# Attention values of the later batches: a float32 product with the values stationary in column tiles, and the weights summed on GpSimd

## The chip, the cores and the metric

The kernel runs on one core of a Trainium2 chip. The metric is device time in microseconds (us) for one execution: 2009.07 us before the change, the median of three runs (2008.14 to 2009.09). PE is the matrix engine (TensorE), ACT is ScalarE, DVE is VectorE, POOL is GpSimd, and SP is the queue that issues the transfers.

## The reference, cut to what matters

Four batches of 12480 tokens with 128 channels each. 49 agents first attend to all keys, and then every query attends to the 49 agents:

```python
a2k = softmax(scale * agents @ k.T)      # 49 x 12480, per batch
agent_v = a2k @ v                        # 49 x 128
q2a = softmax(scale * q @ agents.T)      # 12480 x 49
x = q2a @ agent_v                        # tokens x 128
out = (relu(x @ w_in) ** 2) @ w_out      # w_in 128 x 2048, w_out 2048 x 128
```

A softmax subtracts the row's maximum and divides by the sum of the exponentials plus 1e-9. The change is in `a2k @ v` and in the sum of the exponentials that belongs to it, for batches 1 to 3.

## The kernel before

Everything is done transposed: channels or agents on partitions, tokens along the free dimension. `agent_v @ w_in` is one table of 49 x 2048 per batch (`tables`, L327), so that a token's hidden row is its 49 query weights times the table. Tables, weights and hidden values are split into a high and a low float32r part, so that products of float32r come out with float32 accuracy.

**The main loop** (L575) runs over 832 slots. A slot is one eighth of the hidden width for one half (480 tokens) of a block of 960 tokens. Two slots make a pair, and the loop works in pairs. For pair p, counted from 0:

- `first` (L402): PE makes two hidden tiles `h`, one for the even and one for the odd slot, each of two halves of 128 x 480. The pool of `h` has three tiles.
- `hidden` (L420): ACT makes `r` (relu of `h`) and `g_hi` (its square, rounded); DVE multiplies `r` and `h` into `gg`. For an even slot, `gg` is a tile of its own (two of them) and its low part `g_lo = gg - g_hi` is made on POOL in two halves (L433); for an odd slot the product stays in `h` and DVE makes `g_lo`. So the even `h` is free after DVE's `gg`, the odd one after DVE's `g_lo`.
- `second` (L445): the output products, three times two matmuls for each slot (`g_hi` by `wo_hi`, `g_hi` by `wo_lo`, `g_lo` by `wo_hi`), four slots later (`LAG`), that is after `first` of pair p+2.

These instructions are put in a fixed chain for each engine (`queued`, L56). Everything else in the main loop is fed in as steps of two generators and placed between them by a scheduler, which fixes each engine's order when the program is built; at run time each engine works through its own list in order and waits at the head.

- `queries` (L352) makes the query weights of the next block: scores on PE, exponentials, normalisation (`e`, `z`), the split on ACT and POOL (`pp`), four transposes twice (L382).
- `background` (L462) prepares the next batch: `scores` for 13 blocks of keys (12 of 1024 keys, one of 192), `maxima`, then `values` for the same 13 blocks, `gathered`, `tables`. `STEPS` (L481) says how many steps that is, and sets its pace: the steps of a batch are spread over 0.88 of the slots of the batch before.

Small products that don't belong to the main chain write to one single bank of PSUM (`bank`, L156): key scores, query scores, transposes, values and tables follow each other there, and each waits until the one before has been read.

`scores` keeps the scores of a block in a tile `s` of its own (13 tiles, one for each block) and a running maximum in `mx`. `maxima` makes one maximum per agent and spreads it over all partitions (`mb`, L231). `tiled` (L178) is a float32 product whose stationary operand is cut into four column tiles of 32.

`values` (L288), before: POOL subtracts the maximum into `d` (two buffers), ACT takes the exponential, ACT and POOL split the 128 x 392 weights into high and low parts side by side (`e`, two buffers), and the 128 x 1024 values likewise (`vs`, two buffers, with a column of ones for the sum of the weights). PE then multiplies with the weights as the stationary operand (98 columns: both parts) and the values as the moving one (258 columns: both parts and the ones), eight float32r matmuls a block (L303), and DVE adds the result to `av`. `gathered` (L311) adds up the four quarters with a matrix product with `quad`.

Batch 0 has no earlier batch to hide behind. It runs ahead of the main loop with `whole_exps`, `whole_values`, `add_weights` and `whole_sums` (L246 to L286): exponentials in place in `s`, a plain float32 product, the weights summed into `mx` on POOL, and one sum over partitions at the end.

Of the kernel before, what the change touches and what calls it, by code (L numbers as in the profile page):

```python
# [9 lines left out]
F32 = mybir.dt.float32  # L10
F32R = mybir.dt.float32r
U32 = mybir.dt.uint32
AF = mybir.ActivationFunctionType
ALU = mybir.AluOpType
# [3 lines left out]
P = 128  # L18
TP = 120
NT = 8  # L20
# [17 lines left out]
def agent_attention_relu2(ctx: ExitStack, tc: tile.TileContext, qT, kT, v, agT, w_in, w_out, outT):  # L38
    nc = tc.nc
    C, NTOK = qT.shape  # L40
    _, B, NA = agT.shape
    N = NTOK // B
    FF = w_in.shape[1]
# [3 lines left out]
    NK = len(blocks)  # L47
    K2 = 2 * NA
# [3 lines left out]
    scale = 1.0 / math.sqrt(C)  # L52
# [22 lines left out]
    pe, act, dve, pool, sync = (Ordered(e) for e in (nc.tensor, nc.scalar, nc.vector, nc.gpsimd, nc.sync))  # L75

    const = ctx.enter_context(tc.tile_pool(name="const", bufs=1))
    kv = ctx.enter_context(tc.tile_pool(name="kv", bufs=2))
    sp = ctx.enter_context(tc.tile_pool(name="sp", bufs=NK))
    small = ctx.enter_context(tc.tile_pool(name="small", bufs=1))  # L80
# [10 lines left out]
    ident = const.tile([P, P], F32, name="ident")  # L91
# [1 line left out]
    identr = const.tile([TP, TP], F32R, name="identr")  # L93
    nc.scalar.copy(identr, ident[:TP, :TP])

    quad = const.tile([K2, 2, NA], F32, name="quad")
    nc.gpsimd.tensor_copy(quad, ident[:K2, :K2].rearrange("p (h a) -> p h a", h=2))
    for base in (NA, -NA):
        nc.gpsimd.affine_select(
            out=quad.rearrange("p h a -> p (h a)"), in_=quad.rearrange("p h a -> p (h a)"),  # L100
            pattern=[[-1, K2]], compare_op=ALU.not_equal, fill=1.0, base=base, channel_multiplier=1,
        )

    split = [const.tile([P, NT, 2 * (C + 1)], F32R, name=f"vs{i}") for i in range(2)]
    for vs in split:
        nc.gpsimd.memset(vs[:, :, C : C + 1].bitcast(F32), 1.0)
        nc.gpsimd.memset(vs[:, :, 2 * C + 1 :].bitcast(F32), 0.0)
    win = const.tile([C, FF], F32, name="win")
    wo_hi = const.tile([P, NCH, C], F32R, name="wo_hi")
    wo_lo = const.tile([P, NCH, C], F32R, name="wo_lo")  # L110
# [45 lines left out]
    def bank():  # L156
        if alone[0]:
            return ps_h.tile([P, 2, 512], F32, name="h")[:, 0, :]
        return ps_a.tile([P, 512], F32, name="psa")
# [3 lines left out]
    state = {}  # L163

    def load_keys(b, i, pool, name):
        at, rows, nt = blocks[i]
        kt = pool.tile([C, KB], F32, name=name)
        sync.dma_start(kt[:, : rows * nt], kT[:, b * N + at : b * N + at + rows * nt])
        return kt

    def load_values(b, i, pool, name):
        at, rows, nt = blocks[i]
        vt = pool.tile([P, KB], F32, name=name).rearrange("p (t c) -> p t c", c=C)
        src = v[b, at : at + rows * nt, :].rearrange("(p t) c -> p t c", p=rows)
        sync.dma_start(vt[:rows, :nt, :], src)
        return vt

    def tiled(out, stationary, moving):  # L178
        n = stationary.shape[1]
        with tc.high_priority():  # L180
            for at in range(0, n, CT):
                up = min(at + CT, n)
                pe.matmul(out[at:up, :], stationary[:, at:up], moving, start=True, stop=True)  # L183

    def scores(b, i, kt):
        st = state.setdefault(b, {"s": []})
# [27 lines left out]
    def maxima(b):  # L214
        st = state[b]
        m1 = small.tile([P, NA], F32, name="m1")
        dve.reduce_max(m1, st["mx"].rearrange("p t a -> p a t"), axis=AX.X)
        yield
        pt = bank()
        pe.transpose(pt[:NA, :P], m1, ident)  # L220
        yield
        m2 = small.tile([NA, 1], F32, name="m2")
        dve.reduce_max(m2, pt[:NA, :P], axis=AX.X)
        dg = small.tile([NA, NA], F32, name="dg")
        dve.tensor_scalar_mul(dg, ident[:NA, :NA], m2)
        yield
        pb = bank()
        pe.matmul(pb[:, :NA], ones[:NA, :], dg, start=True, stop=True)
        yield
        st["mb"] = small.tile([P, NA], F32, name="mb")  # L230
        dve.tensor_copy(st["mb"], pb[:, :NA])  # L231

    def halves(out, x, n, eng):

        w = x.shape[2]
        act.copy(out[:, :, :w], x)  # L236
        yield
        eng.tensor_sub(out[:, :, n : n + w], x, out[:, :, :w].bitcast(F32))  # L238

    def less_maximum(b, i, out, eng):  # L240
        st = state[b]
        _, rows, nt = blocks[i]
        mb = st["mb"][:rows, :].rearrange("p (o a) -> p o a", o=1).broadcast_to([rows, nt, NA])
        eng.tensor_sub(out, st["s"][i][:rows, :nt, :], mb)

    def whole_exps(b, i, eng):  # L246
        _, rows, nt = blocks[i]
        e = state[b]["s"][i][:rows, :nt, :]
        less_maximum(b, i, e, eng)
        act.activation(e, e, AF.Exp, scale=scale)  # L250
# [14 lines left out]
    def add_weights(b, i):  # L265
        st = state[b]
        _, rows, nt = blocks[i]
        if i > 0:
            es = st["mx"][:rows, :nt, :]
            pool.tensor_add(es, es if i > 1 else st["s"][0], st["s"][i][:rows, :nt, :])  # L270

    def whole_sums(b):
        st = state[b]
        e1 = small.tile([P, 2, NA], F32, name="e1")
        dve.reduce_sum(e1[:, 0, :], st["mx"].rearrange("p t a -> p a t"), axis=AX.X)
        dve.tensor_copy(e1[:, 1, :], e1[:, 0, :])
        yield
        av = st["avT"] = small.tile([C, K2], F32, name="avT")
        act.copy(av[:, :NA], st["pv"][:C, 0, :NA])
        dve.tensor_add(av[:, :NA], av[:, :NA], st["pv"][:C, 1, NA : 2 * NA])  # L280
        dve.tensor_copy(av[:, NA:], av[:, :NA])
        pz = bank()
        pe.matmul(pz[:K2, :1], e1.rearrange("p h a -> p (h a)"), ones[:, :1], start=True, stop=True)
        rl = st["rl"] = small.tile([K2, 1], F32, name="rl")
        dve.tensor_scalar_add(rl, pz[:K2, :1], 1e-9)
        dve.reciprocal(rl, rl)  # L286

    def values(b, i, vt):  # L288
        st = state[b]
        _, rows, nt = blocks[i]  # L290
        d = small.tile([P, NT, NA], F32, name="d", bufs=2)[:rows, :nt, :]
        less_maximum(b, i, d, pool)
        W = 2 * (C + 1)
        vs = split[i % 2]
        yield from halves(vs[:rows, :nt, :], vt[:rows, :nt, :], C + 1, pool)
        yield
        act.activation(d, d, AF.Exp, scale=scale)  # L297
        e = small.tile([P, NT, K2], F32R, name="e2", bufs=2)[:rows, :nt, :]
        yield from halves(e, d, NA, pool)
        yield  # L300
        pv = bank()
        for t in range(nt):
            pe.matmul(pv[:K2, :W], e[:, t, :], vs[:rows, t, :], start=(t == 0), stop=(t == nt - 1))  # L303
        yield
        if i == 0:
            st["av"] = small.tile([K2, W], F32, name="av")
            dve.tensor_copy(st["av"], pv[:K2, :W])
        else:
            dve.tensor_add(st["av"], st["av"], pv[:K2, :W])  # L309

    def gathered(b):  # L311
        st = state[b]
        qd = quad.rearrange("p h a -> p (h a)")
        x = small.tile([K2, C + 1], F32, name="x")
        dve.tensor_add(x, st["av"][:, : C + 1], st["av"][:, C + 1 :])
        yield
        pa = bank()
        pe.matmul(pa[:C, :K2], x[:, :C], qd, start=True, stop=True)
        pe.matmul(pa[:K2, K2 : K2 + 1], qd, x[:, C:], start=True, stop=True)
        yield  # L320
        av = st["avT"] = small.tile([C, K2], F32, name="avT")
        act.copy(av, pa[:C, :K2])
        rl = st["rl"] = small.tile([K2, 1], F32, name="rl")
        dve.tensor_scalar_add(rl, pa[:K2, K2 : K2 + 1], 1e-9)
        dve.reciprocal(rl, rl)

    def tables(b):  # L327
        st = state[b]
# [23 lines left out]
    def queries(g):  # L352
# [6 lines left out]
        for t in range(NT):  # L359
            tiled(sv[:, t, :], qt[:, t * TP : (t + 1) * TP], ag[:, b, :])  # L360
# [101 lines left out]
    def background(b):  # L462

        kt = load_keys(b, 0, kv, "kt")
        for i in range(NK):
            nxt = load_keys(b, i + 1, kv, "kt") if i + 1 < NK else load_values(b, 0, kv, "vt")
            yield from scores(b, i, kt)
            yield
            kt = nxt
        yield from maxima(b)  # L470
        yield
        vt = kt
        for i in range(NK):
            nxt = load_values(b, i + 1, kv, "vt") if i + 1 < NK else None
            yield from values(b, i, vt)
            yield
            vt = nxt
        yield from gathered(b)
        yield from tables(b)

    STEPS = NK * 2 + 5 + NK * 6 + 2 + 3 * (FF // 512)  # L481

    def step(gen):

# [90 lines left out]
    for k in range(total + LAG):  # L575
        if k < total:
            g, c = divmod(k, SLOTS)
            b, i = divmod(g, NB)
            if i == 0 and c == 0 and b + 1 < B:
                todo = background(b + 1)  # L580
                done = 0
            goal = (i * SLOTS + c + 1) * STEPS / (SPREAD * NB * SLOTS)
            while done < goal and step(todo):
# [51 lines left out]
```

## Time and profile before

| | |
|---|---|
| median of 3 runs | 2009.07 us |
| the profiled execution, its own time | 2009.03 us |
| its span, from the first to the last instruction | 2007.2 us |
| mean granted clock of PE | 0.99 |
| first key scores of batch 1, early in the main loop | about 101 us |
| values products of batch 1 begin; those of batch 3 end | 225 us; 1404 us |

The page gives each engine's busy time, the chain of work that ended last, and groups of instructions by line. Where a helper records an instruction (`queued`), its line is that helper's, L59. Names are those of the program without buffer numbers, and `out<-in` says what an instruction writes and reads. A timeline row is start, duration, engine, line, instruction, and in brackets how long the engine had been idle before it and what ended that. In a row of windows the columns after the window and its length are PE, PE's weight loads, DVE, ACT and POOL busy, then the clock, the transfers' share and GB/s. Matmul ends are modelled and run into each other, so distances between starts tell more than durations.

### The profile page before, as it was taken

The numbers are of one execution on the slowest core, as the hardware profiler recorded it, in microseconds if no ns is written. First come the engines' busy times: TensorE is split into PE (matmuls) and PEld (weight loads), VectorE is DVE, ScalarE is ACT, GpSimd is POOL, SyncE is SP. The second block draws the span as 40 slices with busy tenths as digits, with TensorE's granted clock in tenths as the row PEclk, the third lists the DMA queues.
The fourth block names the chain that finished last, engine by engine and source line by source line (L and its number), as shares of the span: only waits on it lengthen the run. The fifth ranks groups of instructions, "written<-read, shape, count | busy, mean of one in ns | idle before, by whom it ended". The sixth has DMA issues, their size and how long they took to land. (4 is left out here: it accounts for less than half of the span.)

```text
span 2007.2 us, 40193 instructions
## 1 busy us (share of the span) xinstructions
PE 1960.0 (98%) x15188; PEld 1492.7 (74%) x15188; DVE 1690.4 (84%) x1843; ACT 1777.6 (89%) x2100; POOL 1272.3 (63%) x1103
## 2 busy tenths in 40 slices
PE   8699999999999999999999999999999999999999
PEld 8477777777777777777777777777777777777777
DVE  5678888888888888888888888888888888888887
ACT  2388999999988999999988899999999999999997
POOL 2555887765555777776555687775565656556555
PEclk8799999999999999999999999999999999999999
DMA  8243121221133121121123121211111111111000
GB/s 312 73 158 94 59 73 63 66 83 38 50 100 93 50 77 51 61 77 50 49 76 89 54 69 58 75 36 40 52 38 45 38 45 38 36 48 38 33 24 20
DMA packets 55976, 131.89 MB, mean 66 GB/s; under 512 B 6712, under 2 KB 35336, under 8 KB 55784
## 3 DMA queue, kind: packets, MB, share of 16 engines
q1 hardware_dynamic: 55784, 129.33, 19.9%
q8 instruction: 120, 1.97, 0.4%
q14 instruction: 72, 0.59, 0.1%
HBM read 80.97 MB, written 25.56 MB: 53 GB/s over the span
## 5 line engine op out<-in xcount | busy, mean ns | idle before, releaser
L433 POOL TENSOR_TENSOR g_lo<-gg,g_hi 128x480 fp32r<-128x480 f32 x832 | 1000.6, 1224 | 645.7 <-DVE gg L59 437.0
L59 ACT ACTIVATE r<-h 128x960 f32<-128x960 f32 x832 | 801.2, 963 | 86.4 <-PE h L59 77.9
L59 ACT ACTIVATE g_hi<-r 128x960 fp32r<-128x960 f32 x832 | 837.6, 1007 | 35.0 <-issue 0.7
L59 DVE TENSOR_TENSOR h<-r,h 128x960 f32<-128x960 f32 x416 | 481.8, 1158 | 152.7 <-ACT r L59 148.9
L59 PE MATMUL o<-g_hi,wo_hi 128*128 128x480 f32 x1664 | 538.6, 405 | 0.0
L59 DVE TENSOR_TENSOR gg<-r,h 128x960 f32<-128x960 f32 x416 | 477.4, 1148 | 47.8 <-ACT r L59 41.0
L59 DVE TENSOR_TENSOR g_lo<-h,g_hi 128x960 fp32r<-128x960 f32 x416 | 480.5, 1155 | 37.7 <-ACT g_hi L59 4.3
L59 PE MATMUL h<-w,aw_hi 128*128 128x480 f32 x1664 | 476.4, 397 | 23.6 <-DVE gg L59 21.7
L59 PE MATMUL o<-g_lo,wo_hi 128*128 128x480 f32 x1664 | 494.3, 378 | 0.0
L59 PE MATMUL o<-g_hi,wo_lo 128*128 128x480 f32 x1664 | 494.2, 378 | 0.0
L59 PEld LDWEIGHTS o<-g_hi,wo_hi 128*128 128x128 f32 x1664 | 280.4, 188 | 118.7 <-issue 62.9
L59 PEld LDWEIGHTS h<-w,aw_hi 128*128 128x128 f32 x1664 | 290.5, 189 | 87.2 <-DVE gg L59 39.1
L59 PEld LDWEIGHTS o<-g_hi,wo_lo 128*128 128x128 f32 x1664 | 312.7, 188 | 47.4
L59 PEld LDWEIGHTS o<-g_lo,wo_hi 128*128 128x128 f32 x1664 | 312.5, 188 | 46.8
L59 PE MATMUL h<-x,aw_ex 19*128 19x480 f32 x1664 | 205.1, 480 | 0.6 <-DMA x<-w 0.6
L59 PEld LDWEIGHTS h<-x,aw_ex 19*128 19x128 f32 x1664 | 80.2, 182 | 141.3 <-issue 137.4
L59 DVE COPY ob<-o 128x480 f32<-128x480 f32 x104 | 68.2, 656 | 34.7 <-PE o L59 34.7
L238 POOL TENSOR_TENSOR vs<-vt,vs 128x1024 fp32r<-128x1024 f32 (+1 forms) x39 | 81.7, 2095 | 8.7 <-ACT vs L236 8.6
L387 ACT CAST w<-psa 98x480 fp32r<-98x480 f32 x102 | 55.7, 546 | 2.3 <-PE psa L382 0.2
L382 PEld LDWEIGHTS psa<-identr,pp 120*98 120x98 f32 x408 | 51.2, 165 | 8.3
L238 POOL TENSOR_TENSOR pp<-e,pp 120x392 fp32r<-120x392 f32 x51 | 49.2, 966 | 3.3 <-ACT pp L236 3.3
L183 PEld LDWEIGHTS psa<-ag,qt 128*32 128x32 f32 (+1 forms) x3200 | 37.9, 108 | 16.7 <-issue 10.3
(113 smaller groups left out, 986.2 us busy)
## 6 DMA issues: line engine op xcount, KB each, us to landing
qt<-in_qT SPq DMA_DIRECT2D x52, 480.0 KB
out_T<-ob SPq DMA_DIRECT2D x104, 240.0 KB
kt<-in_kT SPq DMA_DIRECT2D x36, 512.0 KB
vt<-in_v SPq DMA_DIRECT2D x36, 512.0 KB
x<-w SPq DMA_DIRECT2D x416, 35.6 KB
ahead<-in_kT SPq DMA_DIRECT2D x12, 512.0 KB
ahead<-in_v SPq DMA_DIRECT2D x12, 512.0 KB
w<-w SPq DMA_DIRECT2D x104, 56.2 KB
```

The source lines that it names most:

```text
L59: ins = issue(*args, **kw)
L183: pe.matmul(out[at:up, :], stationary[:, at:up], moving, start=True, stop=True)
L238: eng.tensor_sub(out[:, :, n : n + w], x, out[:, :, :w].bitcast(F32))
L382: pe.matmul(pt[:K2, t * TP : (t + 1) * TP], pp[:, j * (NT // 2) + t, :], identr, start=True, stop=True)
L387: act.copy(w[:K2, :], pt[:K2, :G])
L433: nc.gpsimd.tensor_sub(lo[:, n, :], gg[:, n, :], hi[:, n, :].bitcast(F32))
```

## The change

For batches 1 to 3, `values` now does what the prelude does for batch 0: the maximum is subtracted in place in `s` on POOL, the exponential is taken in place on ACT, POOL adds the weights of all blocks up in `mx`, and no operand is split. The product is turned round: the values (128 x 128) are the stationary operand in four column tiles of 32, and the 49 weights move, in float32. `whole_sums` ends it, with `gathered`, `quad` and `vs` gone.

```diff
-    def tiled(out, stationary, moving):
+    def tiled(out, stationary, moving, start=True, stop=True):
...
-                pe.matmul(out[at:up, :], stationary[:, at:up], moving, start=True, stop=True)
+                pe.matmul(out[at:up, :], stationary[:, at:up], moving, start=start, stop=stop)
...
-        act.copy(av[:, :NA], st["pv"][:C, 0, :NA])
-        dve.tensor_add(av[:, :NA], av[:, :NA], st["pv"][:C, 1, NA : 2 * NA])
+        if "pv" in st:
+            act.copy(av[:, :NA], st["pv"][:C, 0, :NA])
+            dve.tensor_add(av[:, :NA], av[:, :NA], st["pv"][:C, 1, NA : 2 * NA])
+        else:
+            dve.tensor_copy(av[:, :NA], st["av"])
...
     def values(b, i, vt):
...
-        d = small.tile([P, NT, NA], F32, name="d", bufs=2)[:rows, :nt, :]
-        less_maximum(b, i, d, pool)
-        W = 2 * (C + 1)
-        vs = split[i % 2]
-        yield from halves(vs[:rows, :nt, :], vt[:rows, :nt, :], C + 1, pool)
-        yield
-        act.activation(d, d, AF.Exp, scale=scale)
-        e = small.tile([P, NT, K2], F32R, name="e2", bufs=2)[:rows, :nt, :]
-        yield from halves(e, d, NA, pool)
+        whole_exps(b, i, pool)
+        yield
+        add_weights(b, i)
         yield
         pv = bank()
         for t in range(nt):
-            pe.matmul(pv[:K2, :W], e[:, t, :], vs[:rows, t, :], start=(t == 0), stop=(t == nt - 1))
+            tiled(pv[:C, :NA], vt[:rows, t, :], st["s"][i][:rows, t, :], start=(t == 0), stop=(t == nt - 1))
...
-            dve.tensor_add(st["av"], st["av"], pv[:K2, :W])
+            dve.tensor_add(st["av"], st["av"], pv[:C, :NA])
...
-    def gathered(b):
...
-        yield from gathered(b)
+        yield from whole_sums(b)
...
-    STEPS = NK * 2 + 5 + NK * 6 + 2 + 3 * (FF // 512)
+    STEPS = NK * 2 + 5 + NK * 4 + 1 + 3 * (FF // 512)
```

The scheduler puts the new steps elsewhere than the old ones. POOL at the start of the values of batch 2, before, from just ahead of the first difference to the maximum (`d<-s,mb`); `g_lo` is the main loop's, two rows a pair, `pp` and `e<-e,z` belong to the queries:

```order
L238 TENSOR_TENSOR pp<-e,pp 120x8x49
L433 TENSOR_TENSOR g_lo<-gg,g_hi 128x480 x6
L244 TENSOR_TENSOR d<-s,mb 128x392 x2
L433 TENSOR_TENSOR g_lo<-gg,g_hi 128x480 x2
L238 TENSOR_TENSOR e_8283<-d,e_8283 128x8x49
L238 TENSOR_TENSOR e_8519<-d,e_8519 128x8x49
L244 TENSOR_TENSOR d<-s,mb 128x392 x2
L433 TENSOR_TENSOR g_lo<-gg,g_hi 128x480 x2
```

And the same place in the changed program, from the `g_lo` of pair 122 on; `s<-s,mb` is the difference in place, `mx<-` the sum of the weights (line numbers of the changed file, where L402 is the old L433 and L226 the old L238):

```order
L402 TENSOR_TENSOR g_lo<-gg,g_hi 128x480 x2
L226 TENSOR_TENSOR pp<-e,pp 120x8x49
L232 TENSOR_TENSOR s<-s,mb 128x392 x12
L232 TENSOR_TENSOR s<-s,mb 96x98
L402 TENSOR_TENSOR g_lo<-gg,g_hi 128x480 x2
L258 TENSOR_TENSOR mx<-s 128x392
L402 TENSOR_TENSOR g_lo<-gg,g_hi 128x480 x2
L258 TENSOR_TENSOR mx<-mx,s 128x392
L402 TENSOR_TENSOR g_lo<-gg,g_hi 128x480 x2
```

The differences of all 13 blocks stand in one row ahead of the `g_lo` of pair 123, where two stood between pairs before; after that come the sums, one to three between the `g_lo` of one pair and the next, the last behind pair 129. Batch 3 has the same order 104 pairs later. In batch 1 the run stands between pairs 25 and 26, and the last sum behind pair 33.

DVE around pair 130, before (`gg`, `h<-r,h` and `g_lo` are the main loop's three operations of a pair, `av` the running values, `z` and `e` the queries'):

```order
L59 TENSOR_TENSOR h<-r,h 128x2x480
L370 TENSOR_REDUCE z<-e 120x8
L309 TENSOR_TENSOR av<-av,psa 98x258
L59 TENSOR_TENSOR g_lo<-h,g_hi 128x960
L371 TENSOR_SCALAR z<-z 120x8
L372 RECIPROCAL z<-z 120x8
L59 TENSOR_TENSOR gg<-r,h 128x960
```

And in the changed program, where L263 and L264 are the first two lines of `whole_sums`:

```order
L59 TENSOR_TENSOR h<-r,h 128x2x480
L294 TENSOR_TENSOR av<-av,psa 128x49
L59 TENSOR_TENSOR g_lo<-h,g_hi 128x960
L263 TENSOR_REDUCE e_11596<-mx 128x49
L264 COPY e_11596<-e_11596 128x49
L59 TENSOR_TENSOR gg<-r,h 128x960
```

The sum over the blocks (`e<-mx`), which needs POOL's last `mx`, now stands ahead of `gg` of pair 130 in DVE's list; in batch 1 the same two stand ahead of and behind `gg` of pair 34.

More of the change, by code (lines that the diff above doesn't have):

```diff
@@ L94, in agent_attention_relu2 @@
     nc.scalar.copy(identr, ident[:TP, :TP])
[L96 to L107, printed above, removed]
     win = const.tile([C, FF], F32, name="win")
@@ L302, in values @@
         for t in range(nt):
-            pe.matmul(pv[:K2, :W], e[:, t, :], vs[:rows, t, :], start=(t == 0), stop=(t == nt - 1))
+            tiled(pv[:C, :NA], vt[:rows, t, :], st["s"][i][:rows, t, :], start=(t == 0), stop=(t == nt - 1))
         yield
         if i == 0:
-            st["av"] = small.tile([K2, W], F32, name="av")
-            dve.tensor_copy(st["av"], pv[:K2, :W])
-        else:
-            dve.tensor_add(st["av"], st["av"], pv[:K2, :W])
-    def gathered(b):
[L312 to L315, printed above, removed]
-        yield
[L317 to L325, printed above, removed]
+            st["av"] = small.tile([C, NA], F32, name="av")
+            dve.tensor_copy(st["av"], pv[:C, :NA])
+        else:
+            dve.tensor_add(st["av"], st["av"], pv[:C, :NA])
     def tables(b):
```

## The prediction

> **What bounds the kernel now.** I read the profile in this order: busy times and chain, the waits of the matrix engine (PE), the windows by stage, then the timeline around the changed steps. The page first:
>
> ```profile
> PE 1960.0 (98%) x15188; PEld 1492.7 (74%) x15188; DVE 1690.4 (84%) x1843; ACT 1777.6 (89%) x2100; POOL 1272.3 (63%) x1103
> PE 40%; DVE 3%; issue 1%; ACT 0%; DVEq 0%
> ```
>
> PE works 1960 of 2007.2 us, and the chain that ended last is nearly all PE. The list of who waited for whom, with total, count and longest:
>
> ```profile
> PE h L59 <- DVE gg L59: 21.7, 30, 7.4
> ```
>
> The windows over the three later batches' values stages (PE, PEld, DVE, ACT, POOL):
>
> ```profile
> 220.00:460.00 240.00, 239.19 (x1708) 182.97 (x1708) 203.81 (x226) 227.70 (x278) 185.34 (x157) 1.00 0.22 70
> 700.00:940.00 240.00, 237.65 (x1637) 182.29 (x1636) 204.39 (x222) 225.40 (x267) 176.81 (x148) 1.00 0.20 64
> 1180.00:1460.00 280.00, 277.65 (x1889) 211.93 (x1886) 239.63 (x258) 260.83 (x309) 194.87 (x166) 1.00 0.17 54
> ```
>
> PE idles only 0.81 + 2.35 + 2.35 = 5.5 us there. So ACT and POOL time that the change removes is worth at most those stalls; PE time, and new waits of PE, count in full.
>
> I count in pairs of slots: PE makes the four hidden products of pair p, then the output products of pair p-2. From the start of one pair's output products to the next is a pair's price on PE:
>
> ```profile
> 632.09 0.71 PE L59 MATMUL o<-g_hi,wo_hi 128*128 128x480 f32 x2
> 634.88 0.90 PE L183 MATMUL psa<-ag,kt 128*32 128x49 f32 x64
> 637.19 0.69 PE L59 MATMUL o<-g_hi,wo_hi 128*128 128x480 f32 x2
> ...
> 642.30 0.70 PE L59 MATMUL o<-g_hi,wo_hi 128*128 128x480 f32 x2
> 645.53 0.37 PE L183 MATMUL psa<-ag,kt 128*32 128x49 f32 x12
> 646.89 0.70 PE L59 MATMUL o<-g_hi,wo_hi 128*128 128x480 f32 x2
> ...
> 685.00 0.70 PE L59 MATMUL o<-g_hi,wo_hi 128*128 128x480 f32 x2
> 687.68 0.48 PE L382 MATMUL psa<-identr,pp 120*98 120x120 f32 x4
> 689.43 0.69 PE L59 MATMUL o<-g_hi,wo_hi 128*128 128x480 f32 x2
> 693.52 0.70 PE L59 MATMUL o<-g_hi,wo_hi 128*128 128x480 f32 x2
> 697.60 0.71 PE L59 MATMUL o<-g_hi,wo_hi 128*128 128x480 f32 x2
> 700.31 1.12 PE L303 MATMUL psa<-vs,e 128*98 128x258 f32 x8
> 702.64 0.70 PE L59 MATMUL o<-g_hi,wo_hi 128*128 128x480 f32 x2
> ```
>
> A bare pair costs 4.08 (693.52 to 697.60). With four transposes 4.43, so 0.35 more; with the old values product 5.04, so 0.96; with a block of key scores 5.10, so 1.02; with the tail block's scores 4.59, so 0.51. A float32 product shows two records, so the x64 are 32 matmuls.
>
> **The change on PE.** The new values block is 32 matmuls of 32 stationary columns by 49 moving: the very shape and number of a block of key scores. I price it at 1.02 against 0.96: 36 blocks x 0.06 = 2.2 us. The tail block (8 matmuls instead of 2) is priced from the 0.51 row against a quarter of 0.96: 3 x 0.3 = 0.9. The two products of `gathered` become one small one, a few tenths less. PE: +3 us.
>
> The rows also say where the 1.02 comes from: 26 further matmuls cost 0.51, so 0.0196 each, and 0.39 is paid once per visit. The Trainium skill, "TensorEngine Tiling (Array Packing)", Tiling Modes, says that changing the tiling mode drains the engine although tiles work side by side; the 0.39 agrees. Without a drain, by that page's side by side alone, the sum on PE would be about -12 (a rival, below). Accumulating all eight products on one place costs nothing extra by the old rows: eight took 0.96 there, though each shows 1.12 - 7 x 0.12 = 0.28 from start to end. Bounds for a block against before: -0.33 (no such fixed part: 32 x 0.0196 = 0.63) and +1.3 (each of eight groups of four waits out 0.28 before the next); 0.06 has a row of the same shape.
>
> **ACT and DVE.** Removed from ACT, per block: the copy of the values and of the weights.
>
> ```profile
> L236 ACT CAST vs<-vt 128x1024 fp32r<-128x1024 f32 x36 | 37.4, 1038 | 0.0
> L297 ACT ACTIVATE d<-d 128x392 f32<-128x392 f32 x36 | 18.5, 521 | 0.0
> L236 ACT CAST e<-d 128x392 fp32r<-128x392 f32 x36 | 18.4, 520 | 0.0
> ```
>
> That is 37.4 + 18.4 = 56 us off ACT, and more off POOL, none of it on the chain. What it can give back are stalls like these two, the largest of the second values stage:
>
> ```profile
> 717.02 0.70 PE L59 MATMUL h<-w,aw_hi 128*128 128x480 f32 x2 [0.97 <-DVE gg L59]
> 754.54 0.70 PE L59 MATMUL h<-w,aw_hi 128*128 128x480 f32 x2 [0.94 <-DVE gg L59]
> ```
>
> Recorded idle understates them (matmul ends are modelled), so I raise the 5.5 by about a quarter, an estimate, and take -7 us; bounds 0 and -10. DVE's smaller sums are off the path. The loads of the values stay as many; their buffers now come free at the product instead of the split, for which I charge nothing, a load being asked for a block ahead.
>
> **POOL's order, the main term.** `values` now begins with the difference to the maximum in place. Its 13 tiles have 13 buffers, so nothing holds it back, and the order has all 13 in a row once `mb` is there; the next even slot's `g_lo` queues behind them, and PE, which needs it, behind that. Durations:
>
> ```profile
> L433 POOL TENSOR_TENSOR g_lo<-gg,g_hi 128x480 fp32r<-128x480 f32 x832 | 1000.6, 1224 | 645.7 <-DVE gg L59 437.0 <-ACT r L59 61.6 <-DVE z L370 44.6
> L238 POOL TENSOR_TENSOR pp<-e,pp 120x392 fp32r<-120x392 f32 x51 | 49.2, 966 | 3.3 <-ACT pp L236 3.3
> L244 POOL TENSOR_TENSOR d<-s,mb 128x392 f32<-128x392 f32 x36 | 34.5, 966 | 0.0
> L59 POOL TENSOR_TENSOR mx<-mx,s 128x392 f32<-128x392 f32 x10 | 10.5, 1046 | 0.2
> L59 DVE TENSOR_REDUCE e<-mx 128x49 f32<-128x392 f32 x1 | 0.8, 807 | 0.0
> ```
>
> and where POOL stands against PE within a pair:
>
> ```profile
> 210.57 1.08 PE L59 MATMUL h<-w,aw_hi 128*128 128x480 f32 x4
> 212.98 0.59 PE L59 MATMUL o<-g_lo,wo_hi 128*128 128x480 f32 x2
> 213.18 1.16 DVE L59 TENSOR_TENSOR gg<-r,h 128x960 f32<-128x960 f32 x1 [0.17 <-ACT r L59]
> 214.51 2.38 POOL L433 TENSOR_TENSOR g_lo<-gg,g_hi 128x480 fp32r<-128x480 f32 x2 [1.89 <-DVE gg L59]
> ...
> 216.85 1.88 POOL L244 TENSOR_TENSOR d<-s,mb 128x392 f32<-128x392 f32 x2
> ```
>
> POOL starts a pair's `g_lo` 3.94 after PE starts that pair's hidden tiles; PE reaches the first `g_lo` product 2.41 after a pair's start. Back to back the pieces cost 2.4 (a pair's `g_lo`), 0.95 (a difference), so the run is 12 x 0.95 + 0.4 = 11.8.
>
> Batch 2, pair 122's start as zero. POOL: 3.94 + 2.4 (122) + 0.95 (`pp`) + 11.8 + 2.4 = 21.5 until `g_lo` of pair 123. PE wants it in pair 125: three pairs 12.2, two transposes 0.7, the small maximum product about 0.5 (an estimate from the 0.35 and 0.51), and 2.41 + 0.2: 16.0. A wait of some 5.5 us.
>
> It isn't the whole. The order then gives POOL the weights' sums, one to three per pair, and DVE's `e<-mx` behind the last of them, ahead of `gg` of pair 130; that `gg` frees the hidden tile for pair 131. POOL is busy without a gap: eight pairs' `g_lo` 19.2, `pp` 0.95, run 11.8, twelve sums 11.4 (11 at 0.97, between the 966 and 1046 rows but nearer those of the main loop, and the tail) = 43.4. Then DVE 0.81 + 1.16. In all 3.94 + 43.4 + 1.97 = 49.3. PE wants it at 9 x 4.08 + 0.43 + 3 x 1.02 (two values, one query block) + 0.7 + 0.5 = 41.4. **7.9 us late**, of which 5.5 show at the first wait and the rest at the second. Batch 3 has the same order: 7.9. Batch 1 spreads its sums over two more `pp` and rescale steps and fills part of the first wait with two values blocks and a query block: POOL 9 x 2.4 + 2.8 + 11.8 + 11.4 = 47.6, end 53.5, PE 10 x 4.08 + 0.43 + 4.3 (five blocks, three of them in one visit) + 1.4 + 0.5 = 47.4: 6.1. ACT's 13 exponentials (12 x 0.52 + 0.3 = 6.5 us within two or three pairs) fall into the same waits; without that cover they would cost nearly as much themselves. Sum: 21.9 us. Bounds: differences and sums at 0.85 or at 1.1 each move it by -2.5 or +3.2 a batch: 14 to 32.
>
> **Sum**, on the profiled run's own 2009.03 (span 2007.2 and 1.83 around it; the median is 2009.07): +3 - 7 + 21.9 = +18, **2027 us**. The case's own range, with the bounds of the give-back and of POOL's durations not all at one end: 2017 to 2037.
>
> **Rivals.**
> *The run is hidden (not slower).* If the differences took under about 0.5 us, the run would fit in the slack between making and using `g_lo` (16.0 - 3.94 - 2.4 - 0.95 - 2.4 = 6.3 us, over 13). Then only +3 - 7 = -4 is left: 2005 us. The rows at 966 speak against it; for it, only that the new operation works in place, of which POOL has no row in the main loop at this shape. 0.10.
> *Tiling pays without a drain.* Blocks at 32 x 0.0196 = 0.63 give -12 in place of +3: 2012 us. [...] Against it stands the 0.51 for six matmuls. 0.06.
> *The clock drops as well.* A long idle stretch early in this trace was followed by half speed:
>
> ```profile
> 90.98 0.67 PE L59 MATMUL h<-w,aw_hi 128*128 128x480 f32 x2
> 99.06 1.17 PE L59 MATMUL h<-w,aw_hi 128*128 128x480 f32 x2 [7.41 <-DVE gg L59]
> 108.32 1.00 PE L59 MATMUL o<-g_hi,wo_hi 128*128 128x480 f32 x2
> 109.58 0.59 PE L59 MATMUL o<-g_lo,wo_hi 128*128 128x480 f32 x2
> ```
>
> For 10 us each pair of products took 1.0 instead of 0.6. After a wait of 5.5 that would cost up to 5 us a batch; what POOL's backlog takes anyway (2.4) hides in it, so about +2.5 for two or three batches: 2033 us. The Trainium skill, "TensorE: Matmul & The Clock Gate", Part 1, has half rate after an idle window of about 3.4 us; the 7.41 agrees. 0.12.
>
> **How the numbers follow.** Forecast 0.72, rivals 0.10, 0.06, 0.12. Range 2013 to 2038: it leaves out the hidden run, half of the unpaid drain and the far end of the clock case, under 0.2 in all. A difference of 0.2% (4 us) is what a measurement of this kernel can tell from none. Faster by more: half of the hidden run, 0.05. Within: the other half and most of the unpaid drain, 0.09. Slower: 0.86.
>
> **What would show it.** In the profile after: 13 differences in a row on POOL, three times, about 11.8 us each; PE waiting for POOL's `g_lo` twice for 5 to 6 us, and a few us for DVE's `gg` some 30 us later; a pair with a values block at 5.1; ACT's busy time down by 56. I am wrong if PE's waits for `g_lo` come to under 5 us in all, if a values block costs under 0.8 or over 1.3, or if the granted clock sags after the waits.

## The result and the profile after

The changed kernel took **2029.43 us** (median of 4 runs, 2028.98 to 2030.09) against 2008.85 us before (4 runs, 2008.14 to 2009.09): a ratio of 1.0103, 95% interval 1.0086 to 1.0121. It is slower by 20.6 us. The forecast was 2027.0 us, 18 us slower.

The busy times on the page of the changed kernel:

```profile
PE 1974.4 (97%) x17240; PEld 1488.8 (73%) x17240; DVE 1690.8 (83%) x1852; ACT 1735.2 (86%) x2019; POOL 1190.7 (59%) x1054
```

ACT has 42 us less and POOL 82 us less to do than before, PE 14 us more, and the kernel is slower: the share of busy time says nothing here. (The two groups of casts that went had 57.8 us of records on ACT. The page counts overlapping records once, so its figure falls by less.)

The waits of PE in the changed kernel (in total, times, longest):

```profile
PE h L59 <- DVE gg L59: 13.6, 20, 7.4
PE o L59 <- POOL g_lo L402: 10.4, 4, 4.8
```

The first stood at 21.7 in 30 times before: the many small waits have shrunk. The second is new, and it is where the forecast put it. The windows over the three values stages, PE's busy time in the second column:

```profile
220.00:460.00 240.00, 236.99 (x2305) 178.68 (x2304) 201.13 (x222) 209.04 (x244) 155.26 (x140) 0.99 0.21 68
700.00:940.00 240.00, 239.26 (x2261) 180.14 (x2260) 200.79 (x219) 206.89 (x231) 148.08 (x129) 0.99 0.20 65
1180.00:1460.00 280.00, 274.61 (x2484) 205.40 (x2482) 231.50 (x250) 244.25 (x280) 175.60 (x156) 0.99 0.18 58
```

PE idles 9.1 us in them against 5.5 before, 3.7 us more. The window from 700 us begins just behind the longest wait of the second stage, so the whole program is the better count: the span less PE's busy time is 53.5 us against 47.2, 6.3 us more idle. The other 14 us of the loss are time in which PE counts as busy, most of it on the same products, only slower. The timeline of the second stage shows both (start, duration, engine, line, operation):

```profile
685.22 11.37 POOL L232 TENSOR_TENSOR s<-s,mb 128x392 f32<-128x392 f32 x13
691.87 0.70 PE L59 MATMUL o<-g_hi,wo_hi 128*128 128x480 f32 x2
696.53 2.38 POOL L402 TENSOR_TENSOR g_lo<-gg,g_hi 128x480 fp32r<-128x480 f32 x2
697.81 0.77 PE L59 MATMUL o<-g_lo,wo_hi 128*128 128x480 f32 x1 [4.80 <-POOL g_lo L402]
698.97 0.77 PE L59 MATMUL o<-g_lo,wo_hi 128*128 128x480 f32 x1 [0.39 <-POOL g_lo L402]
699.53 1.00 PE L59 MATMUL o<-g_hi,wo_hi 128*128 128x480 f32 x2
703.55 0.70 PE L59 MATMUL o<-g_hi,wo_hi 128*128 128x480 f32 x2
707.67 0.71 PE L59 MATMUL o<-g_hi,wo_hi 128*128 128x480 f32 x2
710.49 0.91 PE L171 MATMUL psa<-s,vt 128*32 128x49 f32 x64
712.82 0.70 PE L59 MATMUL o<-g_hi,wo_hi 128*128 128x480 f32 x2
...
727.15 0.70 PE L59 MATMUL h<-w,aw_hi 128*128 128x480 f32 x2 [0.74 <-DVE gg L59]
```

The thirteen differences stand in a row for 11.37 us; `g_lo` comes behind them, and PE waits 5.2 us for its two halves. Then each pair of products takes 1.00 instead of 0.70 or 0.60 (half clock) until PE reaches the next pair. The pair takes 703.55 - 691.87 = 11.68 us where a bare one took 4.08: **7.6 us**. The second wait, 30 us later, is only 0.74. The third stage's long pair takes 12.2 us, with waits of 4.78 and 0.40 for `g_lo`. The first stage's takes 12.6 us, with two values blocks and a query block in it. By the prices of before, the three are 5.6 + 7.6 + 8.1 = 21 us over their like.

In the first stage none of PE's recorded waits is for `g_lo`:

```profile
236.69 0.90 PE L171 MATMUL psa<-ag,qt 128*32 128x49 f32 x64 [1.51 <-DVE av L292]
239.05 1.54 PE L171 MATMUL psa<-s,vt 128*32 128x49 f32 x64 [1.46 <-DVE e L334]
240.51 1.17 PE L59 MATMUL o<-g_lo,wo_hi 128*128 128x480 f32 x2
```

The three small products stand ahead of the `g_lo` products there, and the second and third wait until DVE has read the single bank. POOL's `g_lo`, behind its run of 11.39 us, ended at 240.10, just before PE came to it at 240.51. Without those two waits PE would have stood there at about 237.5 (240.51 less 1.51 and 1.46, an estimate) and waited for `g_lo` all the same.

A values block costs (712.82 - 707.67) - (707.67 - 703.55) = 5.15 - 4.12 = 1.03 us.

Something else is in these rows: the bare pair takes 4.12 and not 4.08. The last batch's stage, which the change doesn't touch, shows it best. Two starts of like pairs, twelve blocks of queries apart, before:

```profile
1482.99 0.69 PE L59 MATMUL o<-g_hi,wo_hi 128*128 128x480 f32 x2
1903.79 0.70 PE L59 MATMUL o<-g_hi,wo_hi 128*128 128x480 f32 x2
```

and in the changed kernel:

```profile
1502.02 0.70 PE L59 MATMUL o<-g_hi,wo_hi 128*128 128x480 f32 x2
1924.39 0.71 PE L59 MATMUL o<-g_hi,wo_hi 128*128 128x480 f32 x2
```

420.80 us became 422.37 us, for 96 pairs of the same instructions, small stalls among them. Over all 416 pairs that is 1.57 x 416/96 = 6.8 us, which no step of the forecast had.

### The profile page after: what moved, and what is told of

Its sections match the earlier page's. It is cut to its first block, busy times and chain, and to the rows that moved or that the text cites. A ratio compares the mean times of both kernels' runs of the same rounds, so it can differ in the third digit from the quotient of the medians.

```text
span 2027.9 us, 44144 instructions
## 1 busy us (share of the span) xinstructions
PE 1974.4 (97%) x17240; PEld 1488.8 (73%) x17240; DVE 1690.8 (83%) x1852; ACT 1735.2 (86%) x2019; POOL 1190.7 (59%) x1054
## 5 line engine op out<-in xcount | busy, mean ns | idle before, releaser
L402 POOL TENSOR_TENSOR g_lo<-gg,g_hi 128x480 fp32r<-128x480 f32 x832 | 999.9, 1223 | 737.6 <-DVE gg L59 474.6
L59 DVE TENSOR_TENSOR gg<-r,h 128x960 f32<-128x960 f32 x416 | 478.0, 1149 | 62.1 <-ACT r L59 47.2
L59 PE MATMUL o<-g_lo,wo_hi 128*128 128x480 f32 x1664 | 502.5, 383 | 10.4 <-POOL g_lo L402 10.4
L59 PE MATMUL o<-g_hi,wo_lo 128*128 128x480 f32 x1664 | 499.9, 381 | 0.0
L59 PE MATMUL h<-w,aw_hi 128*128 128x480 f32 x1664 | 475.0, 398 | 15.9 <-DVE gg L59 13.6
L226 POOL TENSOR_TENSOR pp<-e,pp 120x392 fp32r<-120x392 f32 x51 | 49.4, 968 | 22.1 <-ACT pp L224 22.1
L351 PE MATMUL psa<-identr,pp 120*98 120x120 f32 x408 | 49.9, 243 | 0.0
```

The costliest lines, as they stand in the source:

```text
L59: ins = issue(*args, **kw)
L351: pe.matmul(pt[:K2, t * TP : (t + 1) * TP], pp[:, j * (NT // 2) + t, :], identr, start=True, stop=True)
L402: nc.gpsimd.tensor_sub(lo[:, n, :], gg[:, n, :], hi[:, n, :].bitcast(F32))
```

## Experiments

Each ran on a chip beside the kernel before, whose median was 2008.85 to 2009.97 us from one round to another; so a difference between two kernels of different rounds is uncertain by about 1 us. Ratios are to the kernel before, with 95% intervals.

**1. The run broken up: two differences ahead at most.** The tile `late` lies behind all others in memory, so that nothing else moves.

```
-        whole_exps(b, i, pool)
+        e = st["s"][i][:rows, :nt, :]
+        d = late.tile([P, NT, NA], F32, name="d")[:rows, :nt, :]   # bufs=2
+        less_maximum(b, i, d, pool)
+        act.activation(e, d, AF.Exp, scale=scale)
```

> The changed kernel with one thing undone: the difference of a block's weights goes into a tile of its own with two buffers, and ScalarE's exponential reads that and writes the weights' tile, so GpSimd can be at most two differences ahead and the run of thirteen can't form; every sum and product stays. My theory (the run holds up GpSimd's part of the hidden products): the three long pairs (12.6, 11.7 and 12.2 us, 21.9 us more than their neighbours) are gone, GpSimd no longer ends a wait of PE's for more than 1 us, the half clock after each run goes too, and the time is 2029.4 - 21.9 = 2007.5 us, 2004 to 2011. Rival (GpSimd's sums of weights, or the place of the products in PE's order, are what costs, and the run only shows it): the waits move to other pairs of the same batches, and the time stays over 2020 us.

Measured 2026.24 us (1.0082, 1.0068 to 1.0095). My theory fell: the run is gone and the time isn't. PE's wait for `g_lo` is gone too, and a new one stands in its place:

```profile
PE o L59 <- DVE z L344: 8.4, 4, 3.9
```

The timeline of this kernel around the second stage's wait (DVE, PE and POOL together):

```profile
712.37 2.43 POOL L405 TENSOR_TENSOR g_lo<-gg,g_hi 128x480 fp32r<-128x480 f32 x2
714.62 5.31 DVE L343 TENSOR_SCALAR z<-z 120x8 f32<-120x8 f32 x1
714.75 1.88 POOL L232 TENSOR_TENSOR d<-s,mb 128x392 f32<-128x392 f32 x2
716.58 1.01 POOL L258 TENSOR_TENSOR mx<-mx,s 128x392 f32<-128x392 f32 x1
717.55 2.35 POOL L405 TENSOR_TENSOR g_lo<-gg,g_hi 128x480 fp32r<-128x480 f32 x2
720.41 0.19 DVE L344 RECIPROCAL z<-z 120x8 f32<-120x8 f32 x1
720.63 1.14 PE L59 MATMUL o<-g_hi,wo_hi 128*128 128x480 f32 x2 [3.92 <-DVE z L344]
720.68 0.84 POOL L345 TENSOR_TENSOR e<-e,z 120x392 f32<-120x392 f32 x1 [0.77 <-DVE z L344]
721.57 1.00 PE L59 MATMUL o<-g_hi,wo_lo 128*128 128x480 f32 x2
```

POOL now takes differences, sums and `g_lo` in turn, still without a pause. DVE's addition of 1e-9 to 120x8 sums takes 5.31 us, through five of POOL's instructions, and ends when POOL stops at 719.90, because POOL's next instruction needs the reciprocal of that very z. Everything behind it on DVE is late, and PE waits and then works at half clock. So a new theory: DVE's small addition gets through only when POOL pauses.

**2. Seven differences ahead.** As above with `bufs=7`.

> The same with seven buffers for the difference: a run of seven instead of thirteen, then of three. Theory with a threshold (what a run takes is GpSimd's lateness beyond the slack of its half of the hidden products): the run of thirteen took 11.37 us and made PE wait 4.8 us first, so it had some 6.3 us of slack; seven differences at 0.875 us take 6.1 us, so the first wait is under 1 us, the clock does not drop, and the time is within 3 us of the kernel with two buffers (about 2008 us). Rival (every difference in a run costs PE its share, whatever the run's length): 7/13 of 21.9 = 11.8 us stay, about 2019 us.

Measured 2033.15 us (1.0114, 1.0100 to 1.0128): slower than either theory had it, and no faster than the run of thirteen. In the first stage DVE's addition was held for 5.56 us; in the second, PE waited for `g_lo`:

```profile
703.65 0.77 PE L59 MATMUL o<-g_lo,wo_hi 128*128 128x480 f32 x1 [1.68 <-POOL g_lo L405]
704.81 0.77 PE L59 MATMUL o<-g_lo,wo_hi 128*128 128x480 f32 x1 [0.39 <-POOL g_lo L405]
705.38 1.00 PE L59 MATMUL o<-g_hi,wo_hi 128*128 128x480 f32 x2
```

The length of the run alone isn't what sets the cost. Both delays stand where POOL works without a pause, and half clock follows either.

**3. The tiles put back to their old places in memory.** The changed kernel with two tiles that nothing uses; every engine's order stays.

```
+    const.tile([P, 16928 // 4], F32, name="fill0")   # ahead of win
     win = const.tile([C, FF], F32, name="win")
...
         rl = st["rl"] = small.tile([K2, 1], F32, name="rl")
+        if b == 0:
+            small.tile([P, 10784 // 4], F32, name="fill1")
```

> The changed kernel with two tiles that nothing uses, 16,928 and 10,784 bytes per partition, in the places of the tiles that the change removed: every engine's order of instructions is that of the changed kernel, and the feed-forward network's tiles lie at the addresses they had before. Theory (the output products' matmuls start 5 ns further apart, 220.5 instead of 215.3 ns, because their tiles moved in memory): the gaps go back to 215 ns, six of them in each of 416 pairs, with the hidden products' 251 instead of 246 ns against it: 7 to 10 us less, 2019 to 2023 us. Rival (the addresses don't matter, the gaps come from other work beside the products or from run to run): within 1.5 us of 2029.4 us, gaps as in the changed kernel.

Measured 2022.06 us (1.0060, 1.0047 to 1.0074), 7.4 us under the changed kernel's median: as the first theory has it. The same two pair starts:

```profile
1498.34 0.69 PE L59 MATMUL o<-g_hi,wo_hi 128*128 128x480 f32 x2
1919.23 0.70 PE L59 MATMUL o<-g_hi,wo_hi 128*128 128x480 f32 x2
```

420.89 us, the kernel before's figure again. Bare pairs without a stall (within 0.1 us of the median) say the same: on average 4.081 us here and in the kernel before, 4.107 in the changed kernel.

**4. The converse: the kernel before with its tiles moved.** Same order, `quad`, the two `vs` and the four small tiles at the far end of the memory.

```
+    far = ctx.enter_context(tc.tile_pool(name="far", bufs=1, side="right"))
-    quad = const.tile([K2, 2, NA], F32, name="quad")
+    quad = far.tile([K2, 2, NA], F32, name="quad")
```

> The converse: the kernel before with its two const tiles of split values and four small tiles put at the far end of the memory, so that the feed-forward network's tiles lie at the addresses of the changed kernel; every engine's order of instructions is that of the kernel before. If the addresses set the 5 ns: gaps of 220 ns in the output products and 2008.9 + 7 to 10 = 2016 to 2019 us. If not: within 1.5 us of 2008.9 us, gaps of 215 ns.

Measured 2017.14 us (1.0037, 1.0024 to 1.0049), 7.2 us over the kernel before. The stretch:

```profile
1489.26 0.70 PE L59 MATMUL o<-g_hi,wo_hi 128*128 128x480 f32 x2
1911.82 0.71 PE L59 MATMUL o<-g_hi,wo_hi 128*128 128x480 f32 x2
```

422.56 us, and 4.108 for a bare pair. Forth and back agree: where the tiles lie costs 7 us (7.4 and 7.2 by the medians, 8.6 and 7.4 by the ratios). By the bare pairs it would be 0.026 x 416 = 11 us; that smaller stalls take up the rest is likely and not shown. Why these places are slower isn't told by these runs.

**5. Differences and sums paced by the products.** The product and the sum read the two-buffer tile, so that a difference waits for the product two blocks earlier.

```
+        e = late.tile([P, NT, NA], F32, name="d")[:rows, :nt, :]   # bufs=2
+        less_maximum(b, i, e, pool)
+        act.activation(e, e, AF.Exp, scale=scale)
...
-            tiled(pv[:C, :NA], vt[:rows, t, :], st["s"][i][:rows, t, :], ...)
+            tiled(pv[:C, :NA], vt[:rows, t, :], e[:, t, :], ...)
```

> The changed kernel with the weights paced by the products: difference and exponential stand in a tile of two buffers, and the product and GpSimd's sum read that tile, so a difference waits for the product two blocks earlier; sums and products are those of the changed kernel, and the network's tiles lie where they lie there. Theory (what costs is that GpSimd has no pause for some 37 us at the start of each batch's values, in the run of thirteen as in the run that two buffers allowed, and whatever is held by that, g_lo in the one and VectorE's z in the other): no pair over 6 us is left in the batches' values, and the time is 2029.4 - 21.9 = 2007.5 us, 2003 to 2011. Rival (the sums of weights cost PE their time wherever they stand, since GpSimd's part of the hidden products comes later by 2 us in every block): 36 blocks with 0.3 to 0.6 us each, 2018 us or more.

Measured **2006.35 us** (0.9986, 0.9977 to 0.9995): 23.1 us under the changed kernel, and no long pair is left. POOL of this kernel, at the place where the others had no pause:

```profile
696.21 2.41 POOL L408 TENSOR_TENSOR g_lo<-gg,g_hi 128x480 fp32r<-128x480 f32 x2 [1.36 <-DVE gg L59]
698.56 0.96 POOL L232 TENSOR_TENSOR d<-s,mb 128x392 f32<-128x392 f32 x1
700.25 1.04 POOL L288 TENSOR_TENSOR mx<-mx,d 128x392 f32<-128x392 f32 x1 [0.73 <-ACT d L284]
701.25 2.40 POOL L408 TENSOR_TENSOR g_lo<-gg,g_hi 128x480 fp32r<-128x480 f32 x2
706.36 2.39 POOL L408 TENSOR_TENSOR g_lo<-gg,g_hi 128x480 fp32r<-128x480 f32 x2 [2.71 <-DVE gg L59]
```

The brackets are what the others lack: POOL stops in every pair. The 11 us or more that the rival put on the sums of weights isn't there. (The scheduler also places other steps of batches 1 to 3 anew, so the 23.1 us are those of pacing and order together.)

**6. DVE's addition left out, where the differences stood two ahead.** The sums are at least 1, so adding 1e-9 changes no float32 value.

```
-        dve.tensor_scalar_add(z, z, 1e-9)
```

> The kernel in which the difference had a tile of its own with two buffers, without VectorE's addition of 1e-9 to the queries' sums (they are at least 1, so in float32 the addition changes nothing). There that addition of 120x8 took 5.31 us in each batch, to the moment at which GpSimd paused, and 0.15 us elsewhere at the least. Theory (GpSimd without pause holds this form of instruction on VectorE, and PE's wait of 3.9 us and the half clock after it come from that): the three waits go, 2026.2 - 19 = 2007 us, 2004 to 2012. Rival (GpSimd's backlog is what is late, and z only shows it): another instruction of VectorE (the reciprocal behind it) or GpSimd's g_lo ends a wait as long, and the time stays over 2020 us.

Measured 1996.81 us (0.9938, 0.9925 to 0.9950): 29.4 us less than with it, more than the 19 expected. No other wait took its place; the reciprocal behind it isn't held. PE's waits for DVE:

```profile
PE h L59 <- DVE gg L59: 7.6, 2, 7.4
```

Two waits are left of the 18 that this kernel had with the addition (12.6 us), so the small stalls went as well. Counted by pairs, those that take over 0.12 us more than the median of their like came to 31 us with the addition, the long ones among them, and to 2 us without: that is the 29 us.

**7. The same line left out of the kernel before.**

> The kernel before without the same addition of 1e-9 (51 of them, mean 884 ns, 0.15 us where nothing holds them). If the hold by GpSimd makes the kernel's small stalls (26 us in all in pairs that took longer than their like; 0.6 us in every other block of queries of the last batch), most of them go: 1990 to 2000 us. If the hold only moves to the reciprocal, or other work hides it: 2006 to 2011 us.

Measured 1990.62 us (0.9908, 0.9894 to 0.9921). The addition, most of the time held, was taking 18 us from the kernel before, unseen. The group of it there, and PE's waits without it:

```profile
L371 DVE TENSOR_SCALAR z<-z 120x8 f32<-120x8 f32 x51 | 45.1, 884 | 1.0
```

```profile
PE h L59 <- DVE gg L59: 9.9, 6, 6.8
```

A mean of 884 ns for eight elements in a lane was the sign; the one of the first block took 171 ns. Without the line the scheduler places some steps of batches 1 to 3 otherwise, which is a rival for part of the 18 us. In the last batch the order of every engine is the same but for this line, and there the pairs over their like come to 6.8 us with the addition and 0.7 without.

**8. All three: paced, tiles at the old addresses, no addition.**

> The paced kernel with the network's tiles at the addresses of the kernel before and without the addition of 1e-9. By the terms so far: 2029.4 - 21.9 (long pairs) - 7.4 (addresses, as the changed kernel with the filling tiles measured) - up to 13 (the small stalls that the changed kernel still has): 1988 to 2000 us, faster than both kernels. If GpSimd's sums of weights cost PE wherever they stand: 2008 us or more.

Measured **1986.24 us** (0.9886, 0.9872 to 0.9899), 1.1% faster than the kernel before and the fastest of all.

**9. The changed kernel with only that line left out.** The run of thirteen stays.

> The changed kernel without the addition of 1e-9 to the queries' sums, and nothing else: the run of thirteen differences stays. Theory (the run makes GpSimd's own g_lo late, as the prediction had it, and VectorE's held addition has no part in the long pairs): the three long pairs stay at 11 us or more with the first wait on g_lo near 4.8 us, and only the small stalls go: 2029.4 - 10 = 2019 us, 2015 to 2023. Rival (the long pairs need the held addition, as in the kernel whose differences stood two ahead): they go too, 1996 to 2001 us.

Measured 2015.46 us (1.0033, 1.0021 to 1.0045), in the range of the theory:

```profile
PE o L59 <- POOL g_lo L401: 9.1, 4, 4.2
```

The long pairs stay, at 11.2 to 11.4 us. In the second and third stages they come from `g_lo` behind the run, as the forecast had it: the four waits of this row are theirs. In the first stage PE's recorded waits are again for DVE's reading of the bank (1.21 and 1.46 us).

**10. The product turned round, but without column tiles** (on the kernel of 8).

```
-            tiled(pv[:C, :NA], vt[:rows, t, :], e[:, t, :], ...)
+            pe.matmul(pv[:C, :NA], vt[:rows, t, :], e[:, t, :], ...)
```

> The fastest kernel so far (1986.2 us) with the values' product not cut into column tiles: eight products of 128 stationary columns by 49 in each block instead of thirty-two of 32 by 49. What a tiled block takes is about 1.0 us; the first batch's like products, of 98 moving columns, take 0.29 us from start to start. If a plain product costs as much as those, a block costs 2.3 us and 36 blocks 1.3 x 36 = 47 us more (2033 us); if its price goes with the moving columns, 1.2 us and 7 us more (1993 us). If the column tiles bring nothing, 1986 us.

Measured 2012.55 us (1.0018, 1.0009 to 1.0026), 26.3 us more. A pair with a values block in it, plain:

```profile
708.63 0.70 PE L59 MATMUL o<-g_hi,wo_hi 128*128 128x480 f32 x2
711.77 1.88 PE L297 MATMUL psa<-d,vt 128*128 128x49 f32 x16
714.51 0.70 PE L59 MATMUL o<-g_hi,wo_hi 128*128 128x480 f32 x2
```

and tiled:

```profile
698.99 0.70 PE L59 MATMUL o<-g_hi,wo_hi 128*128 128x480 f32 x2
702.21 0.92 PE L172 MATMUL psa<-d,vt 128*32 128x49 f32 x64
704.10 0.70 PE L59 MATMUL o<-g_hi,wo_hi 128*128 128x480 f32 x2
```

5.88 against 5.11 us. Column tiles save 0.77 us a block, 0.77 x 36 = 28 us, so a price between my two guesses. The Trainium skill, "TensorEngine Tiling (Array Packing)", Performance Considerations, has column tiles for a stationary size up to 64, and for a moving size up to 64 together with a swap of the operands. 49 moving columns against 128 stationary ones, without such a swap, is neither case, and in this pair of runs the tiles pay all the same, as long as the other form is this turned product. Against the old values product, of 258 moving columns, the tiles gain nothing (point 1 below).

**11 and 12. Which removed work gave the small stalls back.** To the paced kernel, one instruction like the removed one:

```
+        pool.tensor_sub(x, vt[:rows, :nt, :], vt[:rows, :nt, :])
```

> The paced kernel (2006.4 us) with one instruction of GpSimd added to each of the 39 blocks, of the kind and size of the values' split that the change took away (128x1024, 2.1 us there; it subtracts the values from themselves into a tile that nothing reads). If that split made the small stalls that the change gave back (28 us in the pairs over their like before, 12 us in the paced kernel): 8 to 16 us more, 2014 to 2022 us. If it was ScalarE's rounding of values and weights that made them: within 2 us of 2006.4 us.

and on ACT:

```
+        act.copy(x, vt[:rows, :nt, :])
+        act.copy(late.tile([P, NT, NA], F32, name="y")[:rows, :nt, :], e)
```

> The paced kernel with ScalarE's two instructions of each block added back in kind and size (a copy of 128x1024, 0.99 us before, and of 128x392, 0.50 us, into tiles that nothing reads). If ScalarE's rounding made the small stalls: 8 to 16 us more, 2014 to 2022 us. If GpSimd's split made them: within 2 us of 2006.4 us.

Measured 2101.85 us (1.0462, 1.0447 to 1.0476) and 2098.79 us (1.0447, 1.0433 to 1.0462). Neither answers the question. The added instructions stood on their engines waiting, on ACT for the values' load (73.1 of 73.2 us), on POOL for the load too (52.0 of 116.5 us) and for releases that the profile puts down to PE (58.0):

```profile
L287 POOL TENSOR_TENSOR x<-vt 128x1024 f32<-128x1024 f32 (+1 forms) x39 | 70.1, 1798 | 116.5 <-PE o L59 58.0 <-DMA vt<-in_v 52.0 <-DVE gg L59 6.5
```

```profile
L287 ACT COPY x<-vt 128x1024 f32<-128x1024 f32 (+1 forms) x39 | 38.9, 997 | 73.2 <-DMA vt<-in_v 73.1
```

The kernel before's cast of the same values waited 0.0. So the comparison put back the work and waits that never were there. It stays open how the gain splits between the two engines' removed work.

## Why the prediction was right in sum, point by point

The forecast was 18 us and the result 20.6. The main term, POOL's run, was right in mechanism and size. That the sum came so near is in part luck: one term was missing and another too small, and the two errors went in opposite directions.

**1. PE's work, +3.** Right. With its tiles at the old addresses the new block takes 5.11 us where the old pair took 5.04: 0.07 x 36 = 2.5 us. The three pairs with a tail block add 0.8 (4.58 against 4.32), and the three with the small product at the end of the sums save some 0.6 (4.28 against 4.47 to 4.58). Float32 with column tiles costs what a block of key scores costs, as read from the rows. The rival that tiling pays needed 0.63 a block and is excluded.

**2. Small stalls given back, -7, bounds 0 and -10.** Too small. The three other terms make 23.1 (changed against paced) + 7.3 (addresses, mean of two runs) + 3 = 33.4, so up to 13 us came back. A count by pairs says about the same: those over their like by more than 0.12 us, the three long ones aside, come to 25 us before and 13 us in the changed kernel. 9.4 of these 12 us came back within the values stages (11.2 to 1.8), which is what the forecast spoke of and within its bounds; 1.2 came back in the last batch (6.8 to 5.6), which the change touches by the addresses alone. The step took PE's recorded idle in the three windows, 5.5 us, and raised it by a quarter; by pairs the stalls there were nearly twice that. It also missed one of their causes. In the kernel before 18 us hung on one small addition on DVE that POOL's work holds (experiment 7), and the change took 82 us of work off POOL. How much came that way: without the addition on both sides, the paced kernel at the old addresses is still 4.4 us faster than the one before (1986.24 against 1990.62), with 3 us more work on PE, so some 7 us came back in other ways and the rest through the addition. Which removed work brought the 7 is open (11 and 12). So is how much of the 13 belongs to the addresses: with the tiles put back (experiment 3), the small stalls of the profiled execution, the slowest of its five, came to 19 us and not 13.

**3. POOL's run, +21.9.** Right in size: the long pairs cost 21 us by the trace, and pacing takes 23.1 us away. Its first wait, forecast 5.5 us, measured 5.2 in the second and third stages, and was covered by other waits in the first, as the forecast had it in part; the run, forecast 11.8 us, measured 11.37. The second wait, forecast as 2.4 us, showed 0.74: PE had been at half clock between, so POOL's backlog was worked off under that. In the changed kernel the run itself suffices (experiment 9). Too narrow was the reason: not only the thirteen in a row decide but that POOL has no pause. Broken into twos and with no wait of PE for `g_lo` left, the kernel stays at 2026 us, through DVE (experiments 1 and 6).

**4. The clock.** Named in the forecast as a sign that I'd be wrong, and as a rival at 2033 us. It came, after each of the three waits, and in the second stage the granted clock shows 6.8 us at half speed (windows at 0.90 from 690 to 697 us and 0.61 from 697 to 704), the first two of it still in the wait. It added little: it replaced most of the second wait, as the rival's own sentence on what hides in it would have it, and the rival's remaining 2.5 us a batch did not show (7.6 and a second wait of 0.74 measured in the second batch, against 7.9 forecast without any clock).

**5. What the forecast lacked.** The addresses, +7.3 us, over every pair of the program: shown twice, forth and back (3 and 4).

Of the four terms three were measured by themselves (3, 23.1, 7.3). The 13 is what remains of the 20.6; its own signs are the pairs over their like (25 to 13), the list of waits (21.7 in 30 times to 13.6 in 20) and the pair of runs without the addition.

## What to carry to other kernels

When a change lets an engine take a step earlier than its user needs it, look at what paces that step now; a buffer count that was there for another reason may have been the pacing, and here putting it back was worth 23 us. Before calling removed work worthless, look in the groups for instructions that take five times what the shortest of them takes: another engine may be holding them, and leaving one out, where the result allows it, tells. And when tiles are removed, compare an untouched stage before and after; a difference there can be the memory's layout, and putting the tiles back tells.

## What the runs showed of the hardware that was not expected

- DVE's tensor-scalar addition, 120x8 in the kernel's memory, takes 0.15 us at the least, 0.17 in the first block, and up to 5.56 us while POOL works without a pause (5.31 with five of POOL's instructions in it, experiment 1). DVE's reductions, its reciprocal of the same z (0.19 us) and its sums that read an accumulator bank were not held in the same stretches. The Trainium skill, "SBUF — State Buffer", Who interferes with whom, names tensor-scalar among the operations that can take the port pair that DVE shares with POOL, and has the second one wait until the first finishes. That it is held fits; that it ends with POOL's current instruction doesn't: here five of POOL's instructions went by.
- The place of the network's tiles in memory moves a bare pair of the same instructions from 4.08 to 4.11 us (experiments 3 and 4).
- Half clock came after PE waits as short as 1.68 us with 0.39 us behind it (experiment 2). The Trainium skill, "TensorE: Matmul & The Clock Gate", Part 1, has an idle window of about 3.4 us; the idle that these rows record is shorter, and as matmuls' ends are modelled it may be understated.
